# RWKV-6 and its MLP on one core: the second MLP product of two token tiles by Strassen's scheme

## The chip, the cores and the metric

The kernel runs on one core of one Trainium2 chip. The metric is device time in microseconds (us), the median of several executions. The profile of one execution gives every instruction's start and duration on that core. The engines are named as in the profile: PE (TensorE, matmuls; PEld is its weight load), DVE (VectorE), ACT (ScalarE), POOL (GpSimd) and SP (SyncE, which issues most DMAs).

## What is computed

```python
# r, k, v, w: (4, 8, 768, 48) = batch, heads, time, head_dim; u: (8, 48)
for t in range(S):
    cur = np.einsum('bhd,bhe->bhde', u[None] * kt, vt)
    y[:, :, t] = np.einsum('bhd,bhde->bhe', rt, state + cur)
    state = wt[:, :, :, None] * state + np.einsum('bhd,bhe->bhde', kt, vt)
# y -> x: (4, 768, 384), heads side by side
mu, var = np.mean(x, -1), np.mean((x - mu) ** 2, -1)
xn = (x - mu) / np.sqrt(var + 1e-06) * g_ln
ch = np.maximum(xn @ w_ch1, 0.0) @ w_ch2      # 384 -> 1536 -> 384
out = x + ch
```

A linear recurrence with a decay per time step and channel is followed by a layer norm and a two-layer MLP with a residual. All of it is float32; the MLP's weights arrive as float64 and are converted on the chip.

## The kernel before

The 4 x 768 tokens are cut into eight rounds of 384 tokens (`RN`), and each round has three token tiles of 128 (`TT`) and two units of four heads (`U`). The recurrence of a round is done in six levels (`NLEV`), which double the length of the blocks that are joined. A level is one slot of the main loop; slot number `(rnd - 1) * 6 + lev`. In each slot:

- `quads` makes the level's products on TensorE into `a_ps`, `grow` multiplies decays into the k and r of both units (`rkT`) on VectorE, and `keep` copies the level's blocks out of PSUM with a mask (`A`). Grow waits for the quads of its level, and the quads of the next level wait for grow.
- `states` (level 0 of the round after) and `outputs` (levels 2 and 3) finish a round: `kv` and `y` on TensorE, the chain `s` and the additions `x<-y,vo` on VectorE.
- `moments`, `norm` and `turned_x` do the layer norm of the round before and turn it (`xT_ps`, `xT`); `ends` turns k (`kn_ps`, `kn`) at level 5.
- `stage` and `squares` fetch and turn w, k and r of a coming round: `stage` issues eight DMAs for each unit and tensor into `raw` tiles (four buffers), and `squares` turns them on VectorE (STREAM_TRANSPOSE). `load`, `load_before`, `own_products`, `own_sums` and `own_term` compute the u term from natural-order loads `nat`, with POOL doing most of it from round 3 on and VectorE the sums.

The MLP of round `rnd` (`mlp`) is a generator that yields after every three matrix products; `fill` draws steps from it between the slot's other tasks, so that TensorE always has MLP work in its queue. `UNTIL` says how many steps should be done by the end of each slot. `mlp(rnd)` starts at the end of level 4 of the next round, so its 12 h steps run around the change of rounds and its second products in levels 2 to 4. The last one runs after everything else.

In the first half of `mlp`, twelve `h_ps` tiles of 128 x 384 are made from `w1_sb` and `xT`, and ScalarE's ReLU puts them into twelve tiles `h`. In the second half, for each token tile i, twelve products of `hs[f][:, ts(i, P)]` (128 x 128, the stationary operand) with `w2_sb[:, f, :]` (128 x 384, moving) add up in one PSUM tile `o_ps`. VectorE adds x into a tile `o`, and SP stores it. The PSUM pool `ps_m` has two buffers for `h_ps` and `o_ps`; `ps_t` has two for transposes, and `ps_a` two for a_ps, kv and y.

Nearly all instructions go through `InOrder`, which keeps them in the order of the program on their engine; SP's plain DMAs may be placed by the scheduler. [...] Because a helper records all of them, almost every row of the profile names line 49; rows are told apart by their tiles.

Of the kernel before, what the change touches and what calls it, by code (L numbers as in the profile page):

```python
# [52 lines left out]
def kernel(  # L53
# [16 lines left out]
    SP = nc.sync  # L70
# [26 lines left out]
    p3 = ctx.enter_context(tc.tile_pool(name="p3", bufs=3))  # L97
    p4 = ctx.enter_context(tc.tile_pool(name="p4", bufs=4))
    p6 = ctx.enter_context(tc.tile_pool(name="p6", bufs=6))
    low = ctx.enter_context(tc.tile_pool(name="low", bufs=4))  # L100
    ph = ctx.enter_context(tc.tile_pool(name="ph", bufs=12))
    ps_t = ctx.enter_context(tc.tile_pool(name="ps_t", bufs=2, space=PSUM))
    ps_a = ctx.enter_context(tc.tile_pool(name="ps_a", bufs=2, space=PSUM))
    ps_m = ctx.enter_context(tc.tile_pool(name="ps_m", bufs=2, space=PSUM))
# [12 lines left out]
    def steps(src, q, c):  # L117

        b, f, g = units[q]
        return src[b, ts(g, NH), ds(f * RN + c * P, P)].rearrange("h p d -> p h d")  # L120

    def load(q, which="wkr", eng=SP):
        for nm in which:
            for c in range(TT):
                eng.dma_start(
                    out=nat[nm][q % 2][:, c, :, 0:D],
                    in_=steps({"w": w, "k": k, "r": r}[nm], q, c),
                )

# [139 lines left out]

    raw, rest, fetched, begun, joined = {}, {}, 0, 0, 0  # L270

    held = [ph.tile([P, RN], F32, tag="h", name=f"held{i}") for i in range(FC)]
    LOW = 4

    def fetch(n=1, eng=SPO):
        nonlocal fetched
# [7 lines left out]
    def begin():  # L284
        nonlocal begun
        i = begun
        if i < len(parts) and i - joined < (len(held) if i < len(held) + LOW else LOW):
            words = raw.pop(i)
            lo, hi = words[:, :, 0].bitcast(U32), words[:, :, 1].bitcast(F32)
            if i < len(held):  # L290
                rest[i] = held[i].bitcast(I32)
            else:
                rest[i] = low.tile([P, WC], I32, tag="rest", name=f"rest{i}")
            upper = rest[i].bitcast(F16).rearrange("p (n two) -> p n two", two=2)[:, :, 1]
            ACT.activation(out=parts[i][0], in_=hi, func=AF.Abs, scale=2.0**-16)
            ACT.activation(out=rest[i], in_=lo, func=AF.Copy, scale=2.0**-29)
            ACT.activation(out=upper, in_=hi, func=AF.Copy, scale=2.0**-100)
            begun = i + 1
            fetch()
# [109 lines left out]
    def own_products(q, eng):  # L409
        b, f, g = units[q]  # L410
        rk = st[q]["ruk"] = p1.tile([P, TT, NH, D], F32, tag="rk", name=f"rk{q}")
        eng.tensor_tensor(
            out=rk, in0=nat["k"][q % 2][..., 0:D], in1=nat["r"][q % 2][..., 0:D], op=ALU.mult
        )
        eng.tensor_tensor(
            out=rk, in0=rk,
            in1=u_bc[:, ts(g, NH)][:, None].broadcast_to([P, TT, NH, D]), op=ALU.mult,
        )
        if q >= FIRST * U:
            k1 = nat["w"][0][..., 0:D]  # L420
            eng.tensor_tensor(out=k1, in0=k1, in1=nat["r"][q % 2][..., 0:D], op=ALU.mult)

    def own_sums(q):
        o = st[q]["own"] = p4.tile([P, TT, NH], F32, tag="own", name=f"own{q}")
# [256 lines left out]
    def norm(rnd):  # L681
        b, f = rounds[rnd]
        mv = mvs.pop(rnd)
        rstd = p2.tile([P, TT], F32, tag="rstd", name=f"rstd{rnd}")
        ACT.activation(out=rstd, in_=mv[:, :, 1], func=AF.Sqrt, bias=eps)
        DVE.reciprocal(out=rstd, in_=rstd)
        xns[rnd] = []
        for i in range(TT):
            xn = p3.tile([P, RN], F32, tag="xn", name=f"xn{rnd}_{i}")
            xn = xn.rearrange("p (h d) -> p h d", d=D)  # L690
            xns[rnd].append(xn)
            DVE.tensor_scalar(
                out=xn, in0=xs[b, f][:, i], scalar1=mv[:, i, 0:1],
                scalar2=rstd[:, i : i + 1], op0=ALU.subtract, op1=ALU.mult,
            )
# [13 lines left out]
    def mlp(rnd):  # L709
        b, f0 = rounds[rnd]  # L710
        x, xT, name = xs[b, f0], xTs[rnd], f"{b}_{f0}"
        hs = []
        for f in range(FC):
            converted(KC * (f * P // WC + 1))
            ps = ps_m.tile([P, RN], F32, tag="m", name=f"h_ps{name}_{f}")
            for kc in range(KC):
                PE.matmul(
                    ps, w1_sb[:, kc, ts(f, P)], xT[:, kc, :], start=kc == 0, stop=kc == KC - 1
                )
            hs.append(ph.tile([P, RN], F32, tag="h", name=f"h{name}_{f}"))  # L720
            ACT.activation(out=hs[f], in_=ps, func=AF.Relu)
            yield

        groups = ((0, 1), (2,)) if rnd == 0 else ((0,), (1,), (2,))
        for group in groups:
            ps = {
                i: ps_m.tile([P, H, D], F32, tag="m", name=f"o_ps{name}_{i}") for i in group
            }
            for f0_ in range(0, FC, KC):
                converted(len(parts) - FC + f0_ + KC)  # L730
                for i in group:
                    for f in range(f0_, f0_ + KC):
                        PE.matmul(
                            ps[i].rearrange("p h d -> p (h d)"), hs[f][:, ts(i, P)],
                            w2_sb[:, f, :], start=f == 0, stop=f == FC - 1,
                        )
                    if f < FC - 1 or i != group[-1]:
                        yield
            for i in group:
                o = p2.tile([P, H, D], F32, tag="o", name=f"o{name}_{i}")  # L740
                DVE.tensor_tensor(out=o, in0=ps[i], in1=x[:, i], op=ALU.add)
                SP.dma_start(
                    out=out[b, ds(f0 * RN + i * P, P), :].rearrange("t (h d) -> t h d", d=D),
                    in_=o,
                )
            yield

    MLP_STEPS = FC + TT * (FC // KC)

# [12 lines left out]

    def fill(until, tasks):

        n = int(until) - done
        m = max(n, len(tasks))
        for i in range(m):
            for t in tasks[i * len(tasks) // m : (i + 1) * len(tasks) // m]:  # L770
                t()
            for _ in range((i + 1) * n // m - i * n // m):
                mlp_step()
# [9 lines left out]
    def each(f, *ranges):  # L783
        calls = [()]
        for r_ in ranges:
            calls = [c + (x,) for c in calls for x in r_]
        return [lambda c=c: f(*c) for c in calls]
# [69 lines left out]
    states(u1)  # L857
    product_sums(u1)
    own_term(u1, POOL)
    own_outputs(u0)  # L860
    warm(3, "t")
    outputs(u0)
# [24 lines left out]
    while len(UNTIL) <= 2 * NLEV + NLEV - 2:  # L887
        UNTIL.append(UNTIL[-1] + 3)
    while len(UNTIL) < NR * NLEV:
        UNTIL.append(UNTIL[-1] + MLP_STEPS // NLEV)  # L890
    ahead = [t for nm in "wkr" for t in each(turned, units_of(2), nm, pairs)]
    JOINS, BEGINS = (3, 4, 4, 4, 4, 2), (3, 3, 4, 4, 3)
    for rnd in range(1, NR + 1):
# [3 lines left out]
        for lev in range(NLEV):  # L897
# [17 lines left out]
            if now:  # L915
                if rnd == 1 and lev == 0:
                    totals(rnd, DVE)
                keep(rnd, lev)
            tasks = []
            if rnd == 1:  # L920
                if lev < 2:
                    tasks += each(load, new, "kr"[lev], [SPO])
# [12 lines left out]
            if rnd == 2 and lev == 0:  # L935
# [2 lines left out]
                    out=odd, in_=ident.rearrange("p (q two) -> p q two", two=2)[:, :, 1],  # L938
                    axis=AX.X, op=ALU.add,
                )  # L940
            if rnd == 2 and lev == 2:
                for q in now:
                    tasks += each(own_products, [q], [DVE]) + each(own_sums, [q])
                    tasks += each(load, new[q % U :][:1], "kr")
            if rnd == 2 and lev == 2:
                tasks += each(load_before, new[:1], [k], [0], [SPO]) + each(load_v, new)
                tasks += each(load_before, new[:1], [v], [1], [SPO])
            if rnd == 2 and lev in (3, 4):
                tasks += each(own_term, now[lev - 3 :][:1], [POOL])
            if rnd > 2 and lev == 1:  # L950
                tasks += each(load, new, ["kr"])
            first = 3 if rnd == 2 else 1
            if rnd > 1 and new and first - 1 <= lev < first + 3:
                m = lev - first
                turns = [(new, "w"), (new[:1], "kr"), (new[1:], "kr")]
                if m >= 0:
                    tasks += each(squares, *turns[m], pairs)
                if m < 2:
                    tasks += each(stage, *turns[m + 1], pairs)
            if rnd == 2:  # L960
                if lev == 0:
                    tasks += each(exchanged, old)
# [20 lines left out]
            chain = 3 if rnd == 2 else 4  # L983
            if rnd > 1 and new and lev == chain:
                tasks += each(own_products, new[:1], [POOL])
            if rnd > 1 and new and lev == chain + 1:
                if lev < NLEV - 1:
                    tasks += each(own_sums, new[:1])
                else:
                    own_sums(new[0])  # L990
                tasks += each(load_before, new[1:], [k], [0])
                tasks += each(own_term, new[:1], [POOL])
                tasks += each(load_before, new[1:], [v], [1])
                tasks += each(own_products, new[1:], [POOL])
# [15 lines left out]
            if rnd == 1 and lev < NLEV - 1:  # L1010
# [4 lines left out]
                    each(product_sums, now) if lev == 1 else [],  # L1015
                )
                del ahead[:n]
            fill(UNTIL[slot], tasks)
            if lev == (2 if rnd == 2 else 4) and old:
                mlps.append(mlp(rnd - 1))  # L1020
    while mlp_step():
# [31 lines left out]
```

## Time and profile before

| | |
|---|---|
| median of 5 executions | 561.44 us (559.73 to 563.61) |
| profiled execution, its time | 559.73 us |
| its span, first to last instruction | 558.0 us |
| granted TensorE clock | 0.999 |
| PE / DVE / ACT / POOL busy | 540.8 / 334.7 / 168.8 / 135.9 us |

Busy time is the time in which an engine had at least one instruction in flight. A matmul's duration in the rows is its latency; matmuls that follow each other overlap, so their pace is read from starts or from the chain of waits. A line of a timeline has start, length, engine, operation, output<-inputs, shapes, how many, and in brackets how long the engine sat idle before it and what it waited for. The profile's round numbers are not shown; the rounds can be told apart by the two y groups that each one has.

### The profile page before, as it was taken

To read this page: it belongs to the slowest core of one execution; us is meant where nothing else is said; L and a number is where in the kernel's file an instruction comes from. 1 tells how busy PE (TensorE), PEld (TensorE's weight loads), DVE (VectorE), ACT (ScalarE), POOL (GpSimd) and SP (SyncE) were. 2 spreads that over 40 slices of the span, in tenths; PEclk is the share of its full clock that TensorE was granted. 3 is DMA by queue.
4 is the path that set the end of the run, shared out by engine and by line. 5 is a ranking of instruction groups with operands and counts; after the bars stand their busy time and mean duration, and the time that the engine had idled before them with its cause. 6 is when DMAs were issued, how large, how long until landed. Compare 5 with 4: busy or idle time off the path is not lost.

```text
span 558.0 us, 18190 instructions
## 1 busy us (share of the span) xinstructions
PE 540.8 (97%) x7898; PEld 354.8 (64%) x7898; DVE 334.7 (60%) x654; ACT 168.8 (30%) x363; POOL 135.9 (24%) x157
## 2 busy tenths in 40 slices
PE   8999999998899999999999999999999999999997
PEld 6776665665556666666666666666666666666554
DVE  4989998769899766665585836666563612030000
ACT  2577877402250024201530124201530034202200
POOL 7140010303583039201770048021830000000000
PEclk9999999999999999999999999999999999999999
DMA  9957787156666566545564647454200000000000
GB/s 231 186 143 144 189 232 187 34 116 121 150 150 137 130 137 142 128 105 116 130 118 122 126 107 150 111 124 102 53 1 18 16 15 1 2 29 15 0 15 28
DMA packets 141552, 56.64 MB, mean 101 GB/s; under 512 B 124448, under 2 KB 130720, under 8 KB 141472
## 3 DMA queue, kind: packets, MB, share of 16 engines
q1 hardware_dynamic: 139600, 54.88, 43.5%
q8 instruction: 62, 1.02, 0.8%
q10 hardware_dynamic: 1872, 0.59, 0.4%
q14 instruction: 18, 0.15, 0.1%
HBM read 48.66 MB, written 4.72 MB: 96 GB/s over the span
## 4 chain that ended last, share of the span: by engine, by line
PE 82%; DVE 8%; ACT 3%; SPq 2%; DMA 2%; issue 2%; POOL 1%; DVEq 0%; POOLq 0%; ACTq 0%
PE o_ps L49 33%; PE h_ps L49 27%; PE a_ps L49 9%; PE y L49 5%; DVE w_sb L49 2%; PE kv L49 2%; DVE rkT L49 2%; PE kn_ps L49 2%; SPq L163 1%; PE xT_ps L49 1%; ACT rest L49 1%; PE own_ps L49 1%; PE k_ps L49 1%; DMA k_runs<-in_k_dram 1%; DMA nat_w<-in_k_dram 1%
## 5 line engine op out<-in xcount | busy, mean ns | idle before, releaser
L49 PE MATMUL h_ps<-xT,w_sb 128*128 128x384 f32 x576 | 196.3, 491 | 2.8 <-DVE o L49 1.4
L49 PE MATMUL o_ps<-w_sb,h 128*128 128x384 f32 x576 | 197.4, 492 | 0.1
L49 PEld LDWEIGHTS h_ps<-xT,w_sb 128*128 128x128 f32 x576 | 105.6, 190 | 70.2 <-DVE o L49 2.0
L49 PEld LDWEIGHTS o_ps<-w_sb,h 128*128 128x128 f32 x576 | 105.4, 190 | 65.2 <-ACT h L49 1.0
L49 DVE TENSOR_TENSOR rkT<-rkT,tot 128x768 f32<-128x768 f32 (+1 forms) x96 | 80.9, 885 | 27.0 <-issue 17.1
L49 ACT ACTIVATE h<-h_ps 128x384 f32<-128x384 f32 x96 | 46.9, 489 | 143.2 <-PE h_ps L49 142.9
L49 PEld LDWEIGHTS a_ps<-rkT 48*64 48x64 f32 x4128 | 64.7, 135 | 22.9 <-issue 11.1
L49 PE MATMUL a_ps<-rkT 48*64 48x32 f32 x4128 | 69.8, 220 | 3.1 <-DVE rkT L49 1.5
L49 DVE TENSOR_TENSOR o<-o_ps,x 128x384 f32<-128x384 f32 x24 | 13.3, 552 | 95.3 <-PE o_ps L49 95.3
L49 POOL TENSOR_TENSOR vo<-v,own 128x576 f32<-128x576 f32 x16 | 20.2, 1262 | 94.0 <-DVE own L49 60.1
L49 ACT ACTIVATE rstd<-mv,eps 128x3 f32<-128x3 f32 x8 | 2.4, 296 | 130.1 <-DVE mv L49 130.1
L49 DVE SCALAR_TENSOR_TENSOR s<-s,decay,kv 128x48 f32<-128x48 f32 x160 | 29.3, 256 | 18.4 <-PE kv L49 18.4
L49 POOL TENSOR_TENSOR nat_w<-nat_w,nat_r 128x576 f32<-128x576 f32 x10 | 14.5, 1449 | 104.9 <-DMA nat_w<-in_v_dram 101.9
L49 DVE COPY_PREDICATED A<-mask,a_ps 128x768 f32<-128x768 int8 x32 | 38.4, 1199 | 0.0
L49 DVE TENSOR_TENSOR x<-y,vo 128x288 f32<-128x288 f32 x32 | 13.1, 452 | 31.3 <-PE y L49 31.3
L49 ACT ACTIVATE xT<-xT_ps,g_sb 128x384 f32<-128x384 f32 x24 | 13.6, 579 | 48.6 <-PE xT_ps L49 48.6
L49 DVE TENSOR_TENSOR rkT<-rkT,wT 128x768 f32<-128x768 f32 x16 | 24.9, 1590 | 0.9 <-PE a_ps L49 0.8
L49 DVE TENSOR_REDUCE own<-rk 128x12 f32<-128x576 f32 x12 | 8.9, 741 | 22.4 <-POOL rk L49 22.4
L49 DVE TENSOR_SCALAR w_sb<-w_sb 128x384 f32<-128x384 f32 (+1 forms) x48 | 19.6, 408 | 0.8
L49 DVE STREAM_TRANSPOSE rkT<-r_runs 128x384 f32<-128x384 f32 x20 | 15.6, 839 | 3.5 <-DMA r_runs<-in_r_dram 3.4
L49 PEld LDWEIGHTS y<-v,A 64*64 64x64 f32 x384 | 12.8, 134 | 7.6 <-issue 4.9
L49 POOL TENSOR_TENSOR rk<-nat_k,nat_r 128x576 f32<-128x576 f32 x10 | 15.7, 1566 | 7.7 <-DMA nat_r<-in_r_dram 4.8
(88 smaller groups left out, 536.0 us busy)
## 6 DMA issues: line engine op xcount, KB each, us to landing
raw<-in_moe_w_ch_dram SPq DMA_DIRECT2D x24, 384.0 KB, 4.1
w_runs<-in_w_dram SPq DMA_DIRECT2D x79, 70.0 KB, 2.1
k_runs<-in_k_dram SPq DMA_DIRECT2D x79, 70.0 KB, 2.0
r_runs<-in_r_dram SPq DMA_DIRECT2D x79, 70.0 KB, 2.1
v<-in_v_dram SPq DMA_DIRECT2D x48, 96.0 KB, 2.8
out_dram<-o SPq DMA_DIRECT2D x24, 192.0 KB, 2.5
nat_r<-in_r_dram SPq DMA_DIRECT2D x42, 96.0 KB, 3.4
nat_k<-in_k_dram SPq DMA_DIRECT2D x42, 96.0 KB, 3.4
```

The lines of the kernel that those rows point to most:

```text
L49: return lambda *args, **kw: self.tc.keep_in_program_order(f(*args, **kw))
L163: eng.dma_start(out=t[ds(HP * j + SQ * e, SQ), 0:n], in_=bass.AP(tensor=src.tensor, offset=first + SQ * e, ap=[[NS * D, SQ], [1, n]]),)
```

## The change

The second products of `mlp(2)` to `mlp(7)` go to a new generator, `seven`. For token tiles 0 and 1 it sees hs as a 2 x 2 matrix of blocks (even or odd f, tile 0 or 1) and w2 as one (even or odd f, left or right 192 columns), and forms the eight block products out of seven, of six products of 192 columns each, by Strassen's scheme. Sums of hs blocks (S2, S3, and two in place) are made by VectorE in each MLP; sums of w2 blocks (`weight_sums`) once, in slots 17 to 19, one of them in place. The third tile is done first, with all 384 columns, in the PSUM tile Z; as the right half of w2's even blocks has had the left half subtracted, the left half of Z is added to x's right half between the even and the odd f. The seven products go to parts of PSUM tiles X, Y and V, from where they are added into x. `hs` and the low words of the conversion become constant tiles, the outputs are added in place into x and stored from there, and xn takes buffers of `scratch` and of tag `kn`. From round 4 on, both units' natural k and r use one buffer (`natural`), since the other holds sums of w2; the second unit's loads are moved to level 4. An MLP has 23 steps rather than 24, spread evenly over the slots. The second unit's squares move to levels 4 and 5; in round 2, stage, squares and the own products are spread over more levels.

```diff
+    def natural(nm, q):
+        return nat[nm][q % 2 if q < 4 * U else 0]
...
+    hs = const.tile([P, FC, RN], F32, name="hs")
+    low = const.tile([P, LOW, WC], F32, name="low")
...
+        if rnd > 1:
+            yield from seven(rnd, x, store)
+            return
...
             for i in group:
-                o = p2.tile([P, H, D], F32, tag="o", name=f"o{name}_{i}")
-                DVE.tensor_tensor(out=o, in0=ps[i], in1=x[:, i], op=ALU.add)
+                DVE.tensor_tensor(out=x[:, i], in0=ps[i], in1=x[:, i], op=ALU.add)
+                store(i)
...
+    M, HD = FC // 2, DM // 2
+    more = const.tile([P, 10, HD], F32, name="more")
+    B_ = w2_sb.rearrange("p (m e) (n d) -> p e n m d", e=2, n=2)
+    A_ = hs.rearrange("p (m e) (i t) -> p e i m t", e=2, t=P)
+    S3, S2 = (low.rearrange("p (i a) (c t) -> p i (a c) t", i=2, t=P)[:, i] for i in range(2))
...
+    def weight_sums(c):
+        if c == 1:
+            DVE.tensor_tensor(out=B_[:, 0, 1], in0=B_[:, 0, 1], in1=B_[:, 0, 0], op=ALU.subtract)
+            return
+        for at, t in pieces(c):
+            n = ds(at, t.shape[1])
+            DVE.tensor_tensor(
+                out=t, in0=more[:, n] if c == 4 else B_[:, 1, 1, n],
+                in1=B_[:, 1, 0, n] if c == 4 else B_[:, 0, 1, n], op=ALU.subtract,
+            )
+
+    def seven(rnd, x, store):
...
+        def product(ps, a_, b_, start, ms=range(M)):
+            for m in ms:
+                PE.matmul(
+                    ps, a_(m), b_(m), start=start and m == 0, stop=True, skip_group_check=True
+                )
+            passed()
...
+        Z = tile_of("z_ps")
+        both = [lambda m, e=e: w2_sb[:, 2 * m + e, :] for e in range(2)]
+        product(Z, A(2, 0), both[0], True, range(M // 2))
+        yield
+        sums(S3, A_[:, 0, 0], A_[:, 0, 1], ALU.subtract)
+        product(Z, A(2, 0), both[0], False, range(M // 2, M))
+        add(2, 1, Z[:, 0:HD])
+        passed()
+        yield
+        sums(A_[:, 0, 1], A_[:, 0, 1], A_[:, 1, 1], ALU.add)
+        X = tile_of("x_ps")[:, 0:HD]
+        product(X, A(0, 0), B(0, 0), True)
+        yield
+        add(0, 0, X)
+        sums(S2, A_[:, 0, 1], A_[:, 0, 0], ALU.subtract)
+        product(Z, A(2, 1), both[1], False, range(M // 2))
+        yield
+        product(Z, A(2, 1), both[1], False, range(M // 2, M))
+        yield
+        due.append(lambda: DVE.tensor_tensor(out=x[:, 2], in0=Z, in1=x[:, 2], op=ALU.add))
+        due.append(lambda: store(2))
+        V = ps_t.tile([P, RN], F32, tag="t", name=f"v_ps{rnd}")
+        product(V[:, 0:HD], A(0, 1), B(1, 0), True)
+        yield
+        product(V[:, HD:], A(1, 1), lambda m: T(4, m), False)
+        add(0, 0, V[:, 0:HD])
+        add(1, 0, V[:, HD:], ALU.subtract)
+        passed()
+        yield
+        sums(A_[:, 1, 0], A_[:, 1, 0], S2, ALU.subtract)
+        product(X, lambda m: S2[:, m], lambda m: T(2, m), False)
+        add(0, 1, X)
+        passed()
+        yield
+        Y = tile_of("y_ps")[:, 0:HD]
+        product(Y, A(1, 0), B(0, 1), True)
+        add(1, 1, Y)
+        passed()
+        yield
+        product(X, lambda m: S3[:, m], lambda m: T(3, m), False)
+        yield
+        add(1, None, X)
+        product(Y, A(0, 1), B(1, 1), False)
+        add(0, 1, Y)
+        passed()
+        store(0)
+        store(1)
+        yield
+
+    MLP_STEPS = FC + TT * (FC // KC) - 1
...
-        UNTIL.append(UNTIL[-1] + MLP_STEPS // NLEV)
+        UNTIL.append(UNTIL[-1] + MLP_STEPS / NLEV)
...
-                for q in now:
-                    tasks += each(own_products, [q], [DVE]) + each(own_sums, [q])
-                    tasks += each(load, new[q % U :][:1], "kr")
+            if rnd == 2 and lev in (2, 3):
+                tasks += each(own_products, now[lev - 2 :][:1], [DVE])
+                tasks += each(own_sums, now[lev - 2 :][:1])
+                tasks += each(load, new[lev - 2 :][:1], "kr")
...
+            if slot in (17, 18, 19):
+                tasks += each(weight_sums, ((3,), (1,), (2, 4))[slot - 17])
...
-                tasks += each(load, new, ["kr"])
-            first = 3 if rnd == 2 else 1
...
+                tasks += each(load, new[:1], ["kr"])
+            turns = {
+                2: ("w", "k0 r0"), 3: ("k0", "k1"), 4: ("r0", "r1"), 5: ("k1 r1", ""), 1: ("", "w"),
+            } if rnd == 2 else {
+                0: ("", "w"), 1: ("w", "k0 r0"), 2: ("k0 r0", "k1 r1"), 4: ("k1", ""), 5: ("r1", ""),
+            }
...
             if rnd > 1 and new and lev == chain:
                 tasks += each(own_products, new[:1], [POOL])
+                if rnd > 2:
+                    tasks += each(load, new[1:], ["kr"])
```

## The prediction

> **What bounds the kernel now.** I read the page's engine table and slices first, then the chain of waits, then the timelines of the stretches that the change touches.
>
> ```profile
> PE 540.8 (97%) x7898; PEld 354.8 (64%) x7898; DVE 334.7 (60%) x654; ACT 168.8 (30%) x363; POOL 135.9 (24%) x157
> ...
> PE   8999999998899999999999999999999999999997
> ...
> DVE  4989998769899766665585836666563612030000
> ...
> PE 82%; DVE 8%; ACT 3%; SPq 2%; DMA 2%; issue 2%; POOL 1%; DVEq 0%; POOLq 0%; ACTq 0%
> PE o_ps L49 33%; PE h_ps L49 27%; PE a_ps L49 9%; PE y L49 5%; DVE w_sb L49 2%; PE kv L49 2%; DVE rkT L49 2%; PE kn_ps L49 2%; SPq L163 1%; PE xT_ps L49 1%; ACT rest L49 1%; PE own_ps L49 1%; PE k_ps L49 1%; DMA k_runs<-in_k_dram 1%; DMA nat_w<-in_k_dram 1%
> ```
>
> TensorE is busy 97% of the span and owns 82% of the chain; o_ps, the second MLP product that the change rewrites, is the largest line of it. VectorE has room: 5 to 6 tenths in the middle slices. The chain by time shows that the middle rounds are nothing but TensorE:
>
> ```profile
> 293.50 1.54 PE y L49 x88
> ...
> 356.07 1.54 PE y L49 x96
> ...
> 531.30 23.23 PE o_ps L49 x72
> ```
>
> From one y to the next, 62.57 us, with no idle in between. The last line prices an o_ps matmul: 23.23 / 72 = 0.3226 us (the row's mean of 492 ns is latency, not pace). Each product in the code is two such matmuls, since 36 products give 72.
>
> **The products.** Before, one MLP runs 72 matmuls of 384 columns: 23.23 us. After, the third token tile keeps 24 of them (7.74 us) and Strassen's seven products are 7 x 6 x 2 = 84 matmuls of 192 columns. No row shows 192 columns; the nearest from both sides are 384 (0.3226) and 128:
>
> ```profile
> 392.40 0.82 PE L49 MATMUL kn_ps<-ident,rkT 128*128 128x128 f32 x6
> 393.06 2.10 PE L49 MATMUL h_ps<-xT,w_sb 128*128 128x384 f32 x6
> ```
>
> Six transposes, each with its own 128x128 f32 weight load, take 393.06 - 392.40 = 0.66 us, 0.110 each. The line through 0.110 at 128 and 0.3226 at 384 gives 0.163 at 192. Bounds: 0.161 (half of 0.3226) and 0.190, the duration of one weight load. I take 0.163: 84 x 0.163 = 13.69, with the third tile 21.43, saving 1.80 us per MLP. `seven` serves rounds 2 to 7, six MLPs: **-10.8 us**, all of it on the path, as the middle and end are TensorE end to end.
>
> **What VectorE gets.** Rows that price it:
>
> ```profile
> L49 DVE TENSOR_TENSOR rkT<-rkT,tot 128x768 f32<-128x768 f32 x64 | 61.0, 992 | 23.6 <-issue 17.1 <-PE a_ps L49 6.5
> L49 DVE TENSOR_TENSOR o<-o_ps,x 128x384 f32<-128x384 f32 x24 | 13.3, 552 | 95.3 <-PE o_ps L49 95.3
> L49 DVE TENSOR_TENSOR x<-y,vo 128x288 f32<-128x288 f32 x32 | 13.1, 452 | 31.3 <-PE y L49 31.3
> ```
>
> Per MLP: four sums of 768 on hs and low, 0.95 each (3.8); seven additions of 192 from PSUM and two of 384 in place of three of 384. From 288 (452 ns) and 384 (552 ns) a 192 costs about 0.35, so 7 x 0.35 - 0.55 = 1.9. VectorE gains 5.7 us in a 62.57 us round in which it is busy 39.4. Once only, `weight_sums` sums 4 x 1152 elements: 5.5 us over three slots. None of it costs the path if TensorE never waits for it. I followed the changed program's queue orders through one round with these durations, t = 0 at the end of the first unit's y:
>
> - Second half of Z (needs `add(2, 1, Z)`, since it accumulates onto the half that is read). TensorE: h 2.1, a_ps 1.5, Z 3.9, X 1.95 with a switch 0.2, y 1.5: it asks at 11.2. VectorE leaves its four transposes at 8.6 (302.13 + 1.52 below, y ending at 295.0), then S3 0.9 and the addition 0.3: 9.8. Slack 1.4 us, the smallest inside the MLP.
> - x_ps with S2 asks at 23.1, S2 is ready at 13.4. a_ps of level 4 asks at 20.9, grow is done by 16.1. xT asks at 22.5, xn is done at 20.5. The last y_ps asks at 29.4, A10 - S2 is done at 25.6. X, Y and V have another product between each read and the next write: over 1 us each.
>
> ```profile
> 302.13 1.52 DVE L49 STREAM_TRANSPOSE rkT<-r_runs 128x384 f32<-128x384 f32 x2
> 304.75 0.56 DVE L49 TENSOR_TENSOR o<-o_ps,x 128x384 f32<-128x384 f32 x1 [1.10 <-PE o_ps L49]
> ```
>
> The second line shows that VectorE stood idle 1.10 us just there. So 0; rival 2 has the price if that cover goes. Behind the waiting Z matmul the a_ps of level 3 is queued, and VectorE's grow waits for it in turn, so a delay there would pass down the round. A rule speaks against it: the Trainium skill (SBUF — State Buffer, section SBUF: two separate sides) says that a VectorE operation with two SBUF inputs and a GpSimd operation exclude each other for the whole instruction. All four sums are of that kind. The POOL timeline has nothing from 289.3 until 321.68:
>
> ```profile
> 321.68 1.43 POOL L49 TENSOR_TENSOR nat_w<-nat_w,nat_r 128x576 f32<-128x576 f32 x1 [32.36 <-DMA nat_w<-in_v_dram]
> ```
>
> and the sums fall at 303 to 320.6. By the rule four collisions would cost up to 4 x 1.43 = 5.7 us of VectorE per round and use up the 1.4; by the trace, 0. I take 0.
>
> **What moves.** (a) Steps are spread evenly now, so one h step fewer stands before level 1's a_ps, which comes 1.9 us earlier against VectorE. VectorE's way there (own sums, states, grow of level 0) is paced by POOL: in the trace grow ends 18.9 us after a_ps of level 5 starts; TensorE will ask for its second half at 19.8. Slack 0.9, less up to 0.4 for the second unit's r transposes now running beside POOL: 0. (b) Transposes bunch: in rounds 4 to 6 three kn_ps groups stand in a row on two PSUM buffers, and the third waits for ScalarE. The trace has this in round 7: 456.52 - 455.02 = 1.50 for nine transposes that need 0.99, 0.5 lost. Three rounds 1.5; round 3 has four kn and three xT in a row, 1.0: **+2.5 us** (0.5 to 4). (c) The second unit's k and r share the first's buffer (`natural`), so their six loads wait on SP for POOL's product ending at 323.1; queued behind them are an output store, the next nat_w loads and w_runs, all needed later. Six issues at 0.5 and 3.4 to land: 329.6, against POOL's turn at 334.0. Cover 4.4 us: 0. (d) Round 2 spread. TensorE waits there now:
>
> ```profile
> 134.04 4.14 PE L49 MATMUL h_ps<-xT,w_sb 128*128 128x384 f32 x12 [1.37 <-DVE o L49]
> ...
> 151.32 0.88 PE L49 MATMUL kn_ps<-ident,rkT 128*128 128x128 f32 x6 [1.94 <-DVE rkT L49]
> 152.84 0.52 PE L49 MATMUL kn_ps<-ident,rkT 128*128 128x128 f32 x3 [0.64 <-ACT kn L49]
> ...
> 167.26 0.90 PE L49 MATMUL a_ps<-rkT 48*64 48x32 f32 x48 [1.04 <-DVE rkT L49]
> ```
>
> The first wait stands behind VectorE's own products of both units; the second unit's (0.76 + 1.59 + 0.75) move behind the next mask and four w transposes (2.8) take their place, so it only shrinks to about 1.0. The k and r runs of the first unit are issued about 4.5 us earlier, as only one unit's natural loads stand before them, which removes VectorE's 2.6 us of waiting for r_runs and the 1.94. What is late next is the last line's wait: a_ps of round 3 needs rkT, behind `next` of the second unit, whose nat_w loads are issued some 1.5 us earlier than now. So the stretch gains 1.5, not 5: **-1.5 us** (0 to -5). (e) At the end two stores follow the last addition instead of one, after a shorter addition: **+0.2**. xn in other buffers and in-place x: 0; their readers are done a slot before.
>
> Sum: -10.8 + 2.5 - 1.5 + 0.2 = -9.6. The profiled execution took 559.73 (span 558.0), so 550.1; it lies 1.7 below the median of 561.44, which gives **551.8**.
>
> **Rivals.**
> 1. Weight loads set the pace (slower). LDWEIGHTS shows 190 ns; if a load begins when the matmul before it begins and must end before the next, 192 columns take 0.192 and the MLP 7.74 + 16.13 = 23.87: six times +0.64 instead of -1.80, so 551.8 + 14.6 = 566.4. It decides from 0.184 per matmul, where the sum is 0. For it: the 190 ns and that no row has 192. Against it: kn_ps, and own_ps, whose twelve 192 ns loads take 1.2 us in all. The skill (TensorE: Matmul & The Clock Gate, section LDWEIGHTS) gives columns / 1.2, 107 ns for 128: by the rule the load hides, by the row's duration it doesn't; the spacing of 0.110 sides with the rule. 0.06.
> 2. VectorE runs late by 3 us at Z in each of rounds 4 to 7, beyond its 1.4: 4 x 1.6 = 6.4, so 558.2. For it: VectorE's order has four transposes ahead of the sum. Against it: the 1.10 idle. 0.12.
> 3. The shared k and r buffer: loads late past their 4.4 us hold POOL, own, states, grow and a_ps in rounds 3 to 6. 2 us past it gives 4 x 2 = 8: 559.8. Against it: the 4.4. 0.08.
> 4. The products are not 0.163 apart for a reason of DVE or PSUM that no row shows, half the gain goes: 557. 0.06.
>
> **How the numbers follow.** The forecast has 0.68; its own range is 548.5 to 555, from -5 in round 2 to +4 on transposes. Half a per cent, 2.8 us, is about what a measurement of this kernel can tell from no change: 558.6 to 564.2 is "same". Faster 0.68 + 0.06 + most of rival 2 and some of 3: 0.84. Same 0.08: the rest of those two. Slower 0.08: rival 1 and a worse case of 3. The range to 557.5 and down to 547 leaves out 0.2.
>
> **What would show it.** z_ps x24, and 84 matmuls of 192 per MLP; in the last MLP, alone on TensorE, 21.4 us from first to last instead of 23.23; the round of 62.57 at 61.2; kn_ps with waits of 0.3 on ScalarE; no wait of TensorE on `x<-z_ps`. It is wrong if the last MLP takes over 22.5, if a_ps of level 1 waits for rkT by over 1 us a round, or if round 3's first a_ps is later than 167.

## The result: the products gained what was forecast, and two new waits took most of it

| | before | after |
|---|---|---|
| median | 563.27 us (51 runs, 559.19 to 565.99) | 560.73 us (30 runs, 558.22 to 565.26) |
| ratio of the runs, 95% interval | | 0.9969 (0.9953 to 0.9986) |
| profiled execution, its span | 559.73, 558.0 us | 565.26, 563.5 us |
| granted TensorE clock in it | 0.999 | 0.979 |

The change gained 0.3%, inside the half per cent that the prediction called no change. The forecast was 551.8 against 561.44, a ratio of 0.983. The profiled execution of after is the slowest of its 30 and that of before among the fastest of its 51, so the two profiles are compared stage by stage here, and the sum of the change is read from the medians.

From the page of after, the engine table, two rows of slices and the shares of the chain:

```profile
PE 543.0 (96%) x8114; PEld 390.1 (69%) x8114; DVE 371.6 (66%) x720; ACT 169.3 (30%) x363; POOL 136.3 (24%) x157
...
PE   8999999999997999989999999999999999999997
...
PEclk9797999999997999998999999999999999999999
...
PE 71%; DVE 14%; ACT 6%; DMA 3%; SPq 3%; issue 2%; POOL 1%; DVEq 0%; ACTq 0%; POOLq 0%
```

TensorE's share of the chain fell from 82% to 71% and VectorE's rose from 8% to 14%: somewhere TensorE now waits for VectorE. Slice 13 has a 7 in the PE row and, in the same place, a 7 in the clock row; the clock row of before was all nines.

The products themselves, in the chain of waits at the end of after, where nothing else is on TensorE (start, length, what):

```profile
538.87 3.87 PE z_ps L49 x12
542.74 1.95 PE x_ps L49 x12
...
558.31 1.96 PE y_ps L49 x12
```

Twelve matmuls of 192 columns take 1.95 us, 0.163 each, and the whole group, up to 558.31 + 1.96 = 560.27, takes 560.27 - 538.87 = 21.40 us in place of 23.23. The y lines of the same chain give the rounds:

```profile
118.66 1.54 PE y L49 x96
...
182.87 1.54 PE y L49 x88
...
315.82 1.54 PE y L49 x88
...
377.35 1.54 PE y L49 x96
```

A steady round is 377.35 - 315.82 = 61.53, against 62.57 before. Round 2, from the first line to the second, is 64.21, where the same two y groups of before stand at 113.92 and 174.16, 60.24 apart. All stages, each by the starts of y in the two profiles:

| stage | predicted | profiles |
|---|---|---|
| start to the second y of round 1 | 0 | +4.7 |
| round 2 | -1.5 | +4.0 |
| round 3 | +1.0 | -0.5, and an MLP step left for the end |
| round 4, the first with `seven` in it | -1.3 | +2.9 |
| rounds 5 and 6, each | -1.3 | -1.0 |
| round 7 | -1.8 | -1.6 |
| from its second y to the end | -3.4 | -1.9, with that step in it |
| sum | -9.6 | +5.5 |

The sum, from exact values, is that of these two executions; the medians differ by -2.5. The first line is the clock: it is at half for 6.8 us from 21.8 and for 6.8 us from 42.3 in this execution. In the profile of the last experiment below, which has no half clock there, the stretch ends 0.6 us earlier than before. Round 3 holds six MLP matmuls fewer than before by count of its rows (102 for 108), 1.94 us, which run at the end now: without that shift it is +1.4 there and -3.9 at the end. Rounds 2 and 4 are what the change spoiled.

**Round 2.** SP's queue in its timeline, before:

```profile
131.99 1.55 SPq L125 DMA_DIRECT2D nat_k<-in_k_dram  x3
133.59 1.60 SPq L125 DMA_DIRECT2D nat_r<-in_r_dram  x3
...
142.31 4.19 SPq L163 DMA_DIRECT2D r_runs<-in_r_dram  x8
146.59 3.63 SPq L163 DMA_DIRECT2D k_runs<-in_k_dram  x8
150.32 3.61 SPq L163 DMA_DIRECT2D r_runs<-in_r_dram  x8
154.03 1.64 SPq L174 DMA_DIRECT2D nat_w<-in_k_dram  x3
```

and after:

```profile
143.42 4.09 SPq L165 DMA_DIRECT2D r_runs<-in_r_dram  x8
147.61 0.37 SPq L734 DMA_DIRECT2D out_dram<-x  x1
148.08 2.57 SPq L127 DMA_DIRECT2D nat_k<-in_k_dram  x3
150.69 1.61 SPq L127 DMA_DIRECT2D nat_r<-in_r_dram  x3
152.40 3.69 SPq L165 DMA_DIRECT2D k_runs<-in_k_dram  x8
156.19 4.80 SPq L165 DMA_DIRECT2D r_runs<-in_r_dram  x8
161.09 1.48 SPq L176 DMA_DIRECT2D nat_w<-in_k_dram  x3
```

SP issues nearly without a gap in both. The six natural loads of the second unit, which had stood ahead of the first unit's runs (131.99 to 135.2), stand between the first unit's runs and the second's now (148.08 to 152.3). For nat_w nothing is gained by that: from 14.9 us after the second y of round 1, the same 48 issues stand ahead of it in both kernels, in another order. Counted from that y, nat_w goes out at 161.09 - 118.59 = 42.5 us, before at 154.03 - 113.86 = 40.2: 2.3 later. The 48 issues took 27.6 us here and 25.3 before; in the five profiles below that keep the new order on SP they took 26.3 to 27.5, and 26.2 in the one with the old order put back. So the new order never brought the load forward. The lateness lies in longer issues, for a reason that stays open. What hangs on it, in the timeline of after:

```profile
165.12 1.43 POOL L49 TENSOR_TENSOR nat_w<-nat_w,nat_r 128x576 f32<-128x576 f32 x1 [5.47 <-DMA nat_w<-in_k_dram]
...
166.58 0.75 DVE L49 TENSOR_REDUCE next<-nat_w 128x12 f32<-128x576 f32 x1 [2.06 <-POOL nat_w L49]
...
169.59 3.76 DVE L49 TENSOR_TENSOR rkT<-rkT,wT 128x768 f32<-128x768 f32 x2
...
171.36 1.02 PE L49 MATMUL a_ps<-rkT 48*64 48x32 f32 x48 [3.50 <-DVE rkT L49]
...
174.84 8.03 PE L49 MATMUL o_ps<-w_sb,hs 128*128 128x384 f32 x18
```

POOL waits 5.47 for the load, VectorE 2.06 for POOL with the states and the grow queued behind, and TensorE 3.50 for the grow. The last line shows a second price: 18 matmuls took 8.03 where before had 6.07. The windows of after around it (stretch, length, PE busy, granted clock, DMA share, GB/s):

```profile
168.00:172.00 4.00, 0.64 (x45) 1.00 0.60 155
172.00:178.80 6.80, 5.77 (x73) 0.50 0.56 113
178.80:182.80 4.00, 4.00 (x14) 1.00 0.25 59
```

TensorE was busy 0.64 of 4 us, and then its clock stood at half for 6.8 us. The +4.0 of this round is made of both: a_ps of the second unit starts 54.8 us after the y, 1.4 later than before's 53.4, and the other 2.6 come behind it, at half clock.

**Round 4.** The chain of waits in after:

```profile
240.53 0.55 DVE more L49
241.08 2.64 DVE wT L49 x4
...
250.08 2.02 DMA r_runs<-in_r_dram
...
253.86 0.27 DVE x L49
```

The weight sums of slot 19 (`more`, 3.9 us with the two ahead of it) stand ahead of the four w transposes. These empty the staging buffers, so the k and r runs are issued late; VectorE waits for r_runs, and the first Z addition, `x<-z_ps`, is late by 2.28 us, as TensorE's timeline has it:

```profile
254.18 3.75 PE L49 MATMUL z_ps<-w_sb,hs 128*128 128x384 f32 x6 [2.28 <-DVE x L49]
```

By the lengths, about 1 us of this is an encounter with POOL, in the timelines of after:

```profile
237.00 1.41 POOL L49 TENSOR_TENSOR rk<-rk,u_bc 128x576 f32<-128x576 f32 x1
...
237.24 2.38 DVE L49 TENSOR_TENSOR more<-w_sb 128x1152 f32<-128x1152 f32 x1
```

The same sum takes 1.35 us in the second experiment below, where POOL is idle. Again the matmuls behind it, 3.75 us for six of 0.32 each, ran at half clock (3.4 us from 253.9).

### The profile page after: what moved, and what is told of

The parts are those of the page before. It is cut to its first block, busy times and chain, and to the rows that moved or that the text cites. A ratio compares the mean times of both kernels' runs of the same rounds, so it can differ in the third digit from the quotient of the medians.

```text
span 563.5 us, 18693 instructions
## 1 busy us (share of the span) xinstructions
PE 543.0 (96%) x8114; PEld 390.1 (69%) x8114; DVE 371.6 (66%) x720; ACT 169.3 (30%) x363; POOL 136.3 (24%) x157
## 4 chain that ended last, share of the span: by engine, by line
PE 71%; DVE 14%; ACT 6%; DMA 3%; SPq 3%; issue 2%; POOL 1%; DVEq 0%; ACTq 0%; POOLq 0%
PE h_ps L49 21%; PE a_ps L49 9%; PE z_ps L49 8%; PE o_ps L49 7%; PE x_ps L49 6%; DVE rkT L49 4%; PE y L49 4%; PE y_ps L49 4%; PE v_ps L49 4%; DVE w_sb L49 2%; ACT low L49 1%; SPq L165 1%; PE kv L49 1%; DVE s L49 1%; DVE A L49 1%
## 5 line engine op out<-in xcount | busy, mean ns | idle before, releaser
L49 PE MATMUL h_ps<-xT,w_sb 128*128 128x384 f32 x576 | 198.7, 493 | 2.2 <-DVE x L49 0.9
L49 ACT ACTIVATE hs<-h_ps 128x384 f32<-128x384 f32 x96 | 46.9, 488 | 160.1 <-PE h_ps L49 159.3
L49 PEld LDWEIGHTS a_ps<-rkT 48*64 48x64 f32 x4128 | 67.1, 139 | 23.6 <-issue 13.1
L49 PE MATMUL z_ps<-w_sb,hs 128*128 128x384 f32 x144 | 52.0, 507 | 2.3 <-DVE x L49 2.3
L49 PE MATMUL o_ps<-w_sb,hs 128*128 128x384 f32 x144 | 52.1, 510 | 0.1
L49 PEld LDWEIGHTS z_ps<-w_sb,hs 128*128 128x128 f32 x144 | 27.0, 195 | 19.0 <-DVE x L49 2.4
L49 DVE SCALAR_TENSOR_TENSOR s<-s,decay,kv 128x48 f32<-128x48 f32 x160 | 29.3, 257 | 14.9 <-PE kv L49 14.9
L49 PEld LDWEIGHTS o_ps<-w_sb,hs 128*128 128x128 f32 x144 | 27.0, 196 | 17.4 <-issue 1.8
L49 DVE TENSOR_TENSOR low<-hs 128x768 f32<-128x768 f32 x12 | 11.5, 962 | 21.5 <-ACT hs L49 21.5
L49 PE MATMUL y_ps<-w_sb,hs 128*128 128x192 f32 x144 | 25.4, 326 | 0.0
L49 PEld LDWEIGHTS y_ps<-w_sb,hs 128*128 128x128 f32 x144 | 23.4, 190 | 0.0
```

Of the source, the lines that this page charges most:

```text
L49: return lambda *args, **kw: self.tc.keep_in_program_order(f(*args, **kw))
```

## The experiments

Each kernel has five to nine runs, whose standard deviation is 1.5 to 2.9 us. By that spread, a difference between two of these kernels is known to some 2 to 3 us, and a difference from after's 30 runs to some 1.5. The 10.8 of the third experiment and the 3.8 of the first stand well clear of this. Of the other differences the sign is fairly sure and the size is not; there the argument rests on the waits in the traces. The ratios are to before's runs beside each kernel; the first four ran on one chip, the last three on another, and before's median was 562.1 on both.

### The order of round 2 put back

```diff
-            if rnd == 2 and lev in (2, 3):
-                tasks += each(own_products, now[lev - 2 :][:1], [DVE])
-                tasks += each(own_sums, now[lev - 2 :][:1])
-                tasks += each(load, new[lev - 2 :][:1], "kr")
+            if rnd == 2 and lev == 2:
+                for q in now:
+                    tasks += each(own_products, [q], [DVE]) + each(own_sums, [q])
+                    tasks += each(load, new[q % U :][:1], "kr")
...
-                2: ("w", "k0 r0"), 3: ("k0", "k1"), 4: ("r0", "r1"), 5: ("k1 r1", ""), 1: ("", "w"),
+                2: ("", "w"), 3: ("w", "k0 r0"), 4: ("k0 r0", "k1 r1"), 5: ("k1 r1", ""),
```

> The changed kernel with the order of round 2 put back: both units' own products and natural loads of k and r in level 2, and the second unit's runs staged and turned one level later, as before. Theory A (SP's queue in round 2 is full, and the spread puts six natural loads ahead of the second unit's k and r runs and of its nat_w loads, so rkT of round 3 comes late and TensorE stands 3.5 and 1.0 us before round 3's second a_ps): the 3.5 goes back to about nothing and the second wait to about 1.0, round 2 takes about 60.2 us from y to y instead of 64.2, and the median falls by 1.3 (the stall alone) to 4 us (if the half clock of 6.8 us that follows the stall goes with it): 556.7 to 559.4. Theory B (the stall comes from the added work on VectorE and not from the order of the loads): the wait stays above 2.5 us and the median within 1 us of 560.7.

Measured: 556.95 us (9 runs), 0.9913 of before (0.9883 to 0.9942). TensorE's waits on rkT ahead of an a_ps are 0.4 us in all, in the whole kernel. In this profile, the slowest of the nine runs, kn_ps waits 3.0 for rkT instead (1.9 before), followed by 3.4 us at half clock, and round 2 takes 61.4 us (expected: 60.2).

So undoing the spread is worth 3.8 us, but the profile doesn't bear out the theory's reason. Counted from the y, the grow of round 3 ends at 53.9 us with the old order put back, and at 53.3 to 54.8 in the three profiles with the new one (after and the next two experiments): the order hardly moves it. With the old order TensorE loses its time earlier, at kn_ps, and asks for a_ps so late that it hardly waits. What goes with the order is the clock: the runs' median granted clock is 0.993 here and 0.985 in after, which is worth some 3 of the 3.8 us by a line fitted to after's runs (0.35 us for each 0.001).

### The weight sums behind the w transposes

```diff
-            if slot in (17, 18, 19):
-                tasks += each(weight_sums, ((3,), (1,), (2, 4))[slot - 17])
+            if slot in (17, 18):
+                tasks += each(weight_sums, ((3,), (1,), (2, 4))[slot - 17])
...
                 tasks += turning
                 turning = []
+            if slot == 19:
+                tasks += each(weight_sums, (2, 4))
```

> The changed kernel with the two last weight sums (3.9 us of VectorE) behind the four w transposes of the same slot instead of ahead of them; nothing else moves. Theory A (the w transposes free the staging buffers, so the sums ahead of them make the k and r runs of that slot late, VectorE waits 2.6 us for them and TensorE 2.3 us for the first Z addition): VectorE's waits for k_runs and r_runs in that stretch go, the wait on x<-z_ps falls from 2.3 to under 0.3, and the median falls by 2.3 to 4 us: 556.7 to 558.4. Theory B (VectorE is late there because of the 5.5 us of weight sums as such): the wait on x<-z_ps stays above 1.5 us and the median within 1 us of 560.7.

Measured: 558.29 us (8 runs), 0.9931 (0.9899 to 0.9962), 2.4 less than after. VectorE's timeline in this kernel:

```profile
232.39 2.98 DVE L49 STREAM_TRANSPOSE wT<-w_runs 128x384 f32<-128x384 f32 x4
235.19 1.35 DVE L49 TENSOR_TENSOR more<-w_sb 128x1152 f32<-128x1152 f32 x1
...
244.29 0.86 DVE L49 STREAM_TRANSPOSE rkT<-r_runs 128x384 f32<-128x384 f32 x1 [0.55 <-DMA r_runs<-in_r_dram]
...
245.87 0.34 DVE L49 TENSOR_TENSOR x<-z_ps,x 128x192 f32<-128x192 f32 x1
```

The waits for the runs fell from 2.57 in all to 0.55, no TensorE wait on z_ps is left, and round 4 takes 61.6 us instead of 65.5. VectorE's operations are the same in both. Two things differ: what their order releases, and the encounter with POOL, which is gone (1.35 us for 2.38). By these lengths some 1.0 us of the wait of 2.28 was the encounter and the rest the order; no run parts them.

### Plain products in the same steps

```diff
-        if rnd > 1:
-            yield from seven(rnd, x, store)
-            return
-
-        for group in ((0,), (1,), (2,)) if rnd else ((0, 1), (2,)):
+        for group in (((0, 1), (2,)), ((0,), (1,), (2,)))[rnd] if rnd < 2 else ((2,), (0,), (1,)):
...
-                    if f < FC - 1 or i != group[-1]:
+                    if (f < FC - 1 or i != group[-1]) and (rnd < 2 or (i, f0_) != (1, KC)):
                         yield
...
-            if slot in (17, 18, 19):
-                tasks += each(weight_sums, ((3,), (1,), (2, 4))[slot - 17])
```

> The changed kernel with the second products of rounds 2 to 7 as 72 plain matmuls of 384 columns, third tile first, in the same 23 steps, and without the weight sums; all moves of loads, squares and round 2 stay. Theory A (the seven products gain 1.80 us in each of six MLPs): 10.8 us come back, and the 2.3 us wait on Z and perhaps the half clock behind it go: 567.5 to 569.2. Theory B (the products gain much less than that over a whole round, since VectorE's added sums or the clock take it back): 561 to 564.

Measured: 569.09 us (6 runs), 1.0115 (1.0078 to 1.0153). Against the kernel of the experiment before, which has no wait on Z either, it is 569.09 - 558.29 = 10.8 us slower: 1.80 for each of six MLPs. That this fits to the tenth is in part luck, given the spread of the runs; the traces carry it. From y to y, a steady round takes 63.36 us here and 61.53 there. The products' gain is whole in the steady rounds, and VectorE's added sums take nothing of it. Without it, the moves alone make before's 62.57 into 63.36, 0.79 a round.

### Three loads moved to ScalarE's queue

On top of the second experiment:

```diff
-                tasks += each(load_before, new[1:], [k], [0])
+                tasks += each(load_before, new[1:], [k], [0], [ACT if rnd == 2 else SP])
```

> The kernel of e2_order with one more move: in round 2 the three nat_w loads of the second unit's k rows go to ScalarE's DMA queue instead of standing behind the r runs on SP. Theory A (SP's queue is what makes nat_w late): POOL's wait of 5.5 us for nat_w goes to under 1, VectorE's next sum no longer waits 2.1 for POOL, TensorE's wait before round 3's second a_ps falls from 3.5 to about 1.5 us, and the median lies 1.5 to 3.5 us below that of e2_order: 554 to 557. Theory B (the r runs, which stay on SP, or VectorE set it): the wait stays above 3 us and the median within 0.7 us of e2_order.

Measured: 556.74 us (6 runs), 0.9874 (0.9833 to 0.9915), 1.5 below the second experiment. The timeline shows why it is not more:

```profile
150.47 1.52 ACTq L49 DMA_DIRECT2D nat_w<-in_k_dram  x3
...
152.04 0.87 ACT L49 ACTIVATE hs<-h_ps 128x384 f32<-128x384 f32 x2 [7.69 <-DMA nat_r<-in_r_dram]
152.59 4.21 PE L49 MATMUL h_ps<-xT,w_sb 128*128 128x384 f32 x6 [3.36 <-ACT hs L49]
```

The a_ps of round 3 no longer waits; about 1.5 us was expected. But the load waits for its buffer, ScalarE's ReLU is queued behind it, and TensorE waits 3.36 us for that ReLU; 6.8 us at half clock follow here too. The wait was moved, not removed, and the grow of round 3 ends 54.1 us after the y, no earlier than in the second experiment (53.3).

### The sums that wait for nat_w moved behind the grow

On top of the second experiment; SP's queue stays as it is:

```diff
                 if rnd >= 2:
-                    tasks += each(own_sums, new[1:]) + each(own_term, new[1:], [POOL])
+                    if rnd > 2:
+                        tasks += each(own_sums, new[1:]) + each(own_term, new[1:], [POOL])
...
+            if rnd == 3 and lev == 0:
+                tasks += each(own_sums, now[1:]) + each(own_term, now[1:], [POOL])
```

> The kernel of e2_order with one move: the second unit's own and next sums of round 2 (VectorE) and its own term (POOL) go from the end of round 2 behind round 3's first grow, so that VectorE no longer waits for POOL's nat_w product ahead of the states and the grow; no load moves. Theory A (the chain nat_w load, POOL product, VectorE next sum, states, grow makes round 3's second a_ps late): TensorE's wait there falls from 2.0 us in e2_order (3.5 in the changed kernel) to under 0.5, no half clock follows it, and the median falls by 2 to 4.5 us against e2_order's 558.3: 554 to 556.3. Theory B (the r runs on SP set the grow): the wait stays above 1.5 us and the median within 1 us of 558.3.

Measured: 555.18 us (6 runs), 0.9862 (0.9821 to 0.9903), 3.1 below the second experiment. The longest wait before round 3's a_ps is 0.82 us (expected: under 0.5), no half clock follows it, and round 2 takes 57.6 us from y to y. This confirms the chain: nat_w is as late on SP as in after (42.4 us after the y), but nobody on the path waits for it, and the grow ends at 50.7 us after the y instead of 53.3. In this profile xT_ps waits 1.15 for xn in round 3 and 3.4 us of half clock follow, which costs that round 2.9 us.

### Matmuls of nothing in the stall

On top of the second experiment:

```diff
+            if (rnd, lev) == (3, 1):
+                warm(18, "t")
             for q in now:
                 if slot and (lev or rnd < FIRST):
```

> The kernel of e2_order with six matmuls of zeros (384 columns, 1.94 us, no one reads them) on TensorE just ahead of round 3's second a_ps, in the time in which it stands there waiting. Theory C (the half clock of 6.8 us that starts there in the profiles is an answer to TensorE standing idle): the y after it comes about 3 us earlier, the rows show a clock of 1.0 there, the median granted clock rises from 0.985 to about 0.991, and the median falls by 2 to 3 us against e2_order's 558.3: 555.3 to 556.3. Theory D (the half clock has another cause, such as the load or chance): the clock drops there all the same, the median stays within 0.7 us of 558.3.

Measured: 556.17 us (6 runs), 0.9899 (0.9872 to 0.9926), 2.1 below the second experiment; the median granted clock is 0.995 instead of 0.985, with all six runs at 0.994 or above where the second experiment's eight lie at 0.981 to 0.994. The second experiment's timeline:

```profile
166.80 1.51 PE L49 MATMUL a_ps<-rkT 48*64 48x32 f32 x48 [2.04 <-DVE rkT L49]
168.85 1.51 PE L49 MATMUL a_ps<-rkT 48*64 48x32 f32 x48 [0.54 <-DVE rkT L49]
170.28 7.73 PE L49 MATMUL o_ps<-w_sb,hs 128*128 128x384 f32 x18
```

and this one's:

```profile
164.99 4.16 PE L49 MATMUL idle<-nought 128*128 128x384 f32 x12
169.08 1.60 PE L49 MATMUL a_ps<-rkT 48*64 48x32 f32 x96
170.61 6.07 PE L49 MATMUL o_ps<-w_sb,hs 128*128 128x384 f32 x18
```

The filler was meant to take 1.94 us and took 3.9, as each f32 product is two matmuls (x12), which the expectation forgot. It even holds a_ps back a little, and the kernel is faster all the same: a_ps and o_ps run at full clock behind it, and the y after them comes 1.6 us earlier (expected: about 3). The half clock is an answer to TensorE standing idle, and no separate mishap. That is shown for this stall; for the others it is argued from their place.

### The kn transposes in pairs again

On top of the experiment with the moved sums, the tasks of level 5 are drawn so that an MLP step follows every second kn group:

```diff
-    def fill(until, tasks):
+    def fill(until, tasks, after=()):
...
+        if after:
+            for t in tasks:
+                t()
+                if t in after[1::2] and n > 0:
+                    mlp_step()
+                    n -= 1
+            tasks = []
...
-            fill(UNTIL[slot], tasks + turning)
+            fill(UNTIL[slot], tasks + turning, kns if rnd > 1 and now and lev == NLEV - 1 else ())
```

> The kernel of e5_sums with the kn transposes of rounds 2 to 6 on TensorE in two pairs with an h step between them, as before the change, instead of three or four groups in a row. Theory A (a third group in a row waits for ScalarE to empty one of two PSUM buffers, some 0.5 us a round): kn_ps's waits on ScalarE, 2.7 us in all, go to about nothing, the steady round falls from 61.5 to about 61.0, and the median lies 1.5 to 2.5 us below e5_sums. Theory B (the wait is hidden or moves to the next switch): within 0.7 us of e5_sums.

Measured: 550.66 us (5 runs), 0.9809 (0.9779 to 0.9838). A steady round takes 61.03. After's timeline in such a round:

```profile
341.03 0.82 PE L49 MATMUL kn_ps<-ident,rkT 128*128 128x128 f32 x6
342.15 0.55 PE L49 MATMUL kn_ps<-ident,rkT 128*128 128x128 f32 x3 [0.30 <-ACT kn L49]
342.53 2.10 PE L49 MATMUL h_ps<-xT,w_sb 128*128 128x384 f32 x6
```

and this kernel's:

```profile
325.89 0.82 PE L49 MATMUL kn_ps<-ident,rkT 128*128 128x128 f32 x6
326.54 2.10 PE L49 MATMUL h_ps<-xT,w_sb 128*128 128x384 f32 x6
328.48 0.82 PE L49 MATMUL kn_ps<-ident,rkT 128*128 128x128 f32 x6
```

The wait of 0.30 and 0.2 of switching are gone, 0.5 a round, 2.5 in five rounds. The median fell by 4.5, more than expected, and only the 2.5 are accounted for; the 2.9 us that the other profile lost at xT_ps did not occur in this one, but what that means for the medians is not shown. This version beats both kernels, before by 1.9% (the ratio above) and after by 1.8% (of its median).

## Why the prediction was wrong

It named the right mechanism for the gain and sized it rightly. It failed in two steps, of which it had set one at a gain and one at nothing, and it lacked a third.

- **The products, -10.8: right.** 0.163 per matmul, 21.40 per MLP for 21.43, and 10.8 us between the second and the third experiment. The rival of the 190 ns weight load is refuted: LDWEIGHTS still shows 190 ns and the pace is 0.163.
- **VectorE's sums against POOL: "by the trace, 0" held for the path in the sums of each MLP, and failed for two weight sums that it did not weigh.** 22 of the 24 sums of 768 took 0.93 to 0.96 us, 21 of them with no POOL row beside them. The other two met POOL and took 1.90 and 1.16 us (at 377 to 381 us), and the round from there is no longer for it (61.54); of the weight sums one took 2.38 for 1.35, as above, and another 1.50 for the 0.55 of a sum of its size without POOL. The rule of the Trainium skill (SBUF — State Buffer, section SBUF: two separate sides) is borne out there.
- **"So 0" for the Z addition, with 1.4 us of slack: wrong once.** In rounds 5 to 7 TensorE never waits for it. In round 4 the slack was used up by `weight_sums`, which the prediction priced at 5.5 us "over three slots" and then added to nothing (the rows have 7.6 us, of which the two encounters with POOL made 2.0). Rival 2 was this wait, at another price: it had it in each of four rounds, and it came in one. The 3.9 us of one slot stood ahead of the transposes that release the staging buffers, and 1.0 of them was the encounter with POOL: TensorE waited 2.28 us for the addition. The second experiment, which removes both, puts the price at 2.4 us.
- **"-1.5" for round 2: wrong, and of the other sign.** The step that failed is "nat_w loads are issued some 1.5 us earlier than now": they are issued 2.3 later in after, and 1.0 to 2.2 later in the five other profiles with that order. The prediction counted the loads that were moved out of the way of the first unit's runs and not that the same six loads still stand ahead of nat_w, behind those runs, on a queue with hardly a gap: 48 issues in the one order as in the other. TensorE asked for round 3's a_ps at 49.3 us after y instead of 51.5, so the forecast gain of 2 us was there, and it only lengthened the wait: a_ps began at 52.8, as the grow came no earlier, and half clock followed. The sign that the prediction had named, a first a_ps of round 3 later than 167, is there: 171.4, of which 4.7 came from the start. The fifth experiment takes VectorE's wait for nat_w off the path; round 2 then takes 57.6 us for before's 60.2, and the median is 3.1 us lower.
- **The clock: not in the sum.** Behind several of TensorE's stalls the rows show its clock at half for 3.4 or 6.8 us. In 16 runs of before the median granted clock was 0.993, in the runs of after 0.985. Over the runs of each kernel by themselves, 0.001 of clock goes with 0.35 (after) and 0.38 us (before) by a fitted line, so 0.008 is some 3 us. With round 2 put back the median clock was 0.993 again, so this loss goes with most of the first experiment's 3.8 us. In the second experiment it stayed at 0.985; a share of the clock in its 2.4 us is not shown. The prediction's base had a clock of 0.999, the upper end of before's runs.
- **Bunching, +2.5: somewhat too small.** 0.79 a round in rounds 4 to 6 where it said 0.5, and 1.4 in round 3 where it said 1.0: 3.8. Of each 0.79, the pairs of kn gave 0.5 back; 0.3 stays unattributed.

Taken together: after 560.7, without the Z wait 558.3, without round 2's wait 555.2, with the kn in pairs 550.7, where each step is known to some 2 or 3 us only. Forecast and measurement, the ratios 0.983 and 0.9969, are some 8 us apart; the Z wait (2.4), the wait of round 2 with its half clock (3.1) and the bunching (1.3) make about 7 of them. The kernel of the fifth experiment is about what the prediction described, with the bunching and without the two waits, and the interval of its ratio (0.9821 to 0.9903) holds the 0.983 of the forecast.

## What to carry to other kernels

Where steps are put in another order on a queue that issues without a gap, count what stands ahead of the load that someone waits for: as long as it is the same set of issues, that load goes out no earlier, however much earlier the first ones are. Price work that is done once in the one slot where it is done, and ask what its engine releases there (buffers, and with them transfers) and not only what the engine's total is. A stall of TensorE of 1 to 3.5 us can cost more than its length, as in several profiles here the clock behind it was halved for 3.4 or 6.8 us. In a kernel that runs 97% busy it can pay to fill a stall with matmuls that no one reads.

## What the hardware showed unexpectedly

The clock fell after stalls of 3.5 us (half for 6.8 us), 3.4 (6.8), 2.3 (3.4) and 2.0 (6.8). It did not fall in the profile of before, where TensorE was busy for 1.24 of the 3.8 us from 149.4; it fell for 3.4 us in the first experiment at the same place, after 0.92 of 3.9. The plainest pair is the wait on Z. In after, above, six matmuls behind a wait of 2.28 us took 3.75 us; in the first experiment, which has this wait too, they took 2.20, at full clock:

```profile
251.10 2.20 PE L49 MATMUL z_ps<-w_sb,hs 128*128 128x384 f32 x6 [2.13 <-DVE x L49]
```

So nearly the same gap may cost something or nothing. The clock goes with much of the spread of these kernels' times: a line fitted through time and clock takes up 0.58 of the variance of after's runs and 0.81 of the 16 of before.

The Trainium skill (TensorE: Matmul & The Clock Gate, section What's actually happening) has the half clock set by a free-running window of about 3.4 us. All stretches at half clock within these profiles are one or two times that, and a window that doesn't start with the gap could explain why equal gaps differ, which no run here shows. Its rule of no idle gaps over some 3 us (section Why this matters for your kernels) would have passed the 2.04 us of the second experiment, which was followed by 6.8 us at half clock. In the last kernel a wait of 1.14 us before round 3's second unit's a_ps was followed by 3.4 us of it. Here the measurement decides: gaps of 1 to 2 us were enough, though not each time.
